# Layer 1 of a kernel's last token group by seven block products in place of eight, with its final output stored by halves

## Chip, cores and metric

One Trainium2 chip, one core. The metric is the device time in microseconds of one execution. All runs that are compared are fast; times are medians, and an interval is the 95% interval of a ratio. A ratio is the mean time of one kernel's fast runs over that of the other's in the same rounds, so it is not quite the ratio of the medians quoted.

The five engines are named as the profile names them: PE (matrix products), PEld (its weight loads), DVE (vector), ACT (scalar, activations), POOL (GpSimd) and SP (which issues most DMAs).

## The reference, cut to what matters

Windowed causal attention on 8 batches of 8 heads and 576 tokens (head size 64), then a normalised two-layer MLP with a residual:

```python
attn = softmax over a window of 64 past positions      # 8 x 8 heads x 576 x 64
x  = attn.transpose(0, 2, 1, 3).reshape(B, S, 512)
xn = (x - mean) / sqrt(var + 1e-6) * g_ln
ch = np.maximum(xn @ w_ch1, 0.0) @ w_ch2               # 512 -> 2048 -> 512
return x + ch
```

## The kernel before

The kernel works on 9 groups of 512 tokens: groups 0 to 7 are the first 512 tokens of each batch, and group 8, the tails' group, holds the last 64 tokens of all 8 batches. While PE computes the MLP of group g, the other engines prepare the attention of the following ones. "Tail i" is the attention of two batches' last 64 tokens; tails 2 and 3 are worked on in group 7. Layer 1 (`l1`) is 16 steps of four 128x512 products each; layer 2 already uses, from group 2 on, seven block products in place of eight (the Strassen-Winograd scheme), for which DVE forms sums `sS` of blocks of the hidden activations `hrT`.

```python
    ps_s = ctx.enter_context(tc.tile_pool(name="pss", bufs=2, space=PSUM))   # 2 banks
    ps_x = ctx.enter_context(tc.tile_pool(name="psx", bufs=1, space=PSUM))   # 2 banks
    ps_t = ctx.enter_context(tc.tile_pool(name="pst", bufs=1, space=PSUM))   # tags t0, t1: 2 banks
    ps_mm = ctx.enter_context(tc.tile_pool(name="psmm", bufs=2, space=PSUM)) # 2 banks
# ... cut ...
    def cast_tail(i):                      # POOL: fp32 -> fp16 of a tail's q, k, v
        # ... cut ...
        nc.gpsimd.memset(vt[:, :, :, D:D + 1], 1.0)
        nc.gpsimd.tensor_copy(out=q16, in_=tq)
        nc.gpsimd.tensor_copy(out=k16, in_=tk)
        nc.gpsimd.tensor_copy(out=vt[:, :, :, 0:D], in_=tv)
# ... cut ...
        def l1(hc):
            hps = ps_mm.tile([128, 512], FP32, tag="mm", name=f"hps_{g}_{hc}")
            for kc in range(NKC):
                nc.tensor.matmul(
                    out=hps, lhsT=w1g[:, kc, 128 * hc:128 * (hc + 1)], rhs=zT[g][:, kc, :],
                    start=(kc == 0), stop=(kc == NKC - 1),
                )
            nc.scalar.activation(out=hrT[:, hc, :], in_=hps, func=AF.Relu, bias=0.0, scale=1.0)
# ... cut: layer 2, products 1 2 6 5 7 4 3, each in two halves p; last one of the last group:
            elif n == 3:
                post("C", 0, 1)
                # ... cut ...
                if last:
                    store_rest(0, slice(256, DM), None)
# ... cut: what runs behind unit i of group g is placed with at(i, function, arguments):
        if len(TAILS.get(g, ())) == 2:     # group 7
            at(3, cast_tail, TAILS[g][1])  # POOL casts tail 3
            at(7, t_tail, TAILS[g][1], 0)  # PE transposes its q, behind layer 1's 8th step
            at(8, t_tail, TAILS[g][1], 1)  # ... and its k
```

In the traces here POOL, DVE and PE run their instructions in the order in which they are written, so a `cast_tail` that is late on POOL stops PE at its transpose, whatever else PE could do (in the changed kernel, below, for 6.87 us).

The softmax here doesn't subtract the row's maximum and nothing guards it: scores larger than these inputs give would overflow.

## Time and profile before

The time before is 314.28 us (3 runs, 313.3 to 314.37). From the page of the profile, first the engines' busy time, then the chain of waits (the work that ended last, followed back), as shares of the span by engine:

```profile
PE 298.9 (95%) x3041; PEld 194.1 (62%) x3041; DVE 205.2 (66%) x385; ACT 153.4 (49%) x258; POOL 166.3 (53%) x251
...
PE 74%; DMA 10%; DVE 7%; SPq 4%; POOL 2%; ACT 1%; issue 1%; POOLq 0%; ACTq 0%
```

PE works 95% of the time, and 74% of the chain is PE's: it is PE that the kernel mostly waits for. The chain in order of time (start, duration, engine, output tile, line, count) shows that group 7's eighth step is followed by the transposes of tail 3's q at 260.13 us, and that the tails' group is PE alone (a piece of the chain starts where the one before it ends; in PE's own timeline, from which the stretches below are taken, tpq starts at 259.97):

```profile
260.13 0.22 PE tpq L245 x4
...
281.35 13.84 PE hps L392 x64
...
305.68 1.76 PE pC L464 x16
...
307.46 0.69 DVE xn L471
```

Layer 1 of the tails' group takes 13.84 us for 64 products, 216 ns each; layer 2 takes 12.25 us for 112 narrower ones, 109 ns each. The POOL timeline (start, duration, engine, line, operation, out<-in, and in brackets the idle time before it) shows where POOL is free, and what stands at the end of that stretch:

```profile
247.81 1.04 POOL L120 CAST vt<-tv 128x1024 f16<-128x1024 f32 x1
258.43 0.17 POOL L117 MEMSET vt<- 128x16 f16 x1 [9.58 <-PE xps L317]
258.56 0.61 POOL L118 CAST tq<-tq 128x512 f16<-128x512 f32 x1
```

POOL idles 9.58 us until 258.43, and then it has 1.7 us to bring tail 3's q to PE at 260.13.

| before, profiled run | us |
|---|---|
| span | 313.0 |
| start to the first product of group 7's layer 1 | 251.99 |
| from there to the transposes of tail 3's q (tpq) | 7.98 |
| from there to the attention products of tail 3 (xps) | 7.51 |
| from there to the end of PE's last product | 39.94 |
| from there to the end (last add, stores) | 5.58 |

### The profile page before, as it was taken

To read this page: it belongs to the slowest core of one execution; us is meant where nothing else is said; L and a number is where in the kernel's file an instruction comes from. 1 tells how busy PE (TensorE), PEld (TensorE's weight loads), DVE (VectorE), ACT (ScalarE), POOL (GpSimd) and SP (SyncE) were. 2 spreads that over 40 slices of the span, in tenths; PEclk is the share of its full clock that TensorE was granted. 3 is DMA by queue.
4 is the path that set the end of the run, shared out by engine and by line. 5 is a ranking of instruction groups with operands and counts; after the bars stand their busy time and mean duration, and the time that the engine had idled before them with its cause. 6 is when DMAs were issued, how large, how long until landed. Compare 5 with 4: busy or idle time off the path is not lost.

```text
span 313.0 us, 7473 instructions
## 1 busy us (share of the span) xinstructions
PE 298.9 (95%) x3041; PEld 194.1 (62%) x3041; DVE 205.2 (66%) x385; ACT 153.4 (49%) x258; POOL 166.3 (53%) x251
## 2 busy tenths in 40 slices
PE   6988998899999999999999999999999999999992
PEld 4457544497554468646964686459646855784582
DVE  1689585855674996589666965896669636751642
ACT  1496633477416752776247526762475058306500
POOL 7578666454760798369814983698145506200000
PEclk9999999999999999999999999999999999999999
DMA  8999999998866996798179997993690393003013
GB/s 192 267 390 290 320 336 272 280 304 184 159 144 196 268 206 105 243 312 147 37 212 316 203 149 219 316 142 67 209 172 19 62 209 117 2 2 134 0 36 101
DMA packets 109892, 57.42 MB, mean 183 GB/s; under 512 B 79841, under 2 KB 100833, under 8 KB 109858
## 3 DMA queue, kind: packets, MB, share of 16 engines
q1 hardware_dynamic: 108944, 54.02, 69.1%
q0 software_dynamic: 768, 2.80, 3.7%
q8 instruction: 24, 0.39, 0.5%
q10 hardware_dynamic: 146, 0.13, 0.1%
q14 instruction: 10, 0.08, 0.1%
HBM read 38.80 MB, written 9.44 MB: 154 GB/s over the span
## 4 chain that ended last, share of the span: by engine, by line
PE 74%; DMA 10%; DVE 7%; SPq 4%; POOL 2%; ACT 1%; issue 1%; POOLq 0%; ACTq 0%
PE hps L392 30%; PE pA L464 11%; PE pC L464 7%; PE pB L464 7%; PE ch L404 6%; DMA w2s<-in_moe_w_ch_dram 4%; DMA qk<-in_k_dram 4%; PE xps L317 3%; PE sc L283 3%; PE hph L513 3%; PE tp L226 2%; SPq L141 2%; DVE sS L443 2%; DMA w1s<-in_moe_w_ch_dram 2%; SPq L89 1%; DVE pt L297 1%
## 5 line engine op out<-in xcount | busy, mean ns | idle before, releaser
L392 PE MATMUL hps<-zT,w1g 128*128 128x512 f16 x480 | 110.4, 379 | 0.0
L396 ACT ACTIVATE hrT<-hps 128x512 f16<-128x512 f32 x120 | 71.9, 599 | 50.7 <-PE hps L392 47.2
L392 PEld LDWEIGHTS <-w1g 128*128 128x128 f16 x480 | 44.6, 98 | 49.3 <-issue 1.0
L290 ACT ACTIVATE pt<-sc 128x512 f16<-128x512 f32 x72 | 39.0, 595 | 29.8 <-DVE xn L471 15.6
L464 PEld LDWEIGHTS <-sS 128*128 128x128 f16 x448 | 43.3, 98 | 5.1
L342 POOL TENSOR_SCALAR rsz<-mvg 128x1 f32<-128x1 f32 x28 | 10.7, 382 | 60.4 <-DVE mvg L328 59.8
L128 POOL CAST qk<-qk 128x1024 f16<-128x1024 f32 x32 | 35.1, 1112 | 13.4 <-DMA qk<-in_q_dram 6.9
L464 PEld LDWEIGHTS <-hrT 128*128 128x128 f16 x336 | 32.6, 98 | 5.2
L212 ACT COPY qkT<-tp 128x1024 f16<-128x1024 f16 x16 | 16.1, 1012 | 35.2 <-PE tp L226 26.1
L297 DVE TENSOR_TENSOR pt<-pt,mask 128x1024 f16<-128x1024 f16 x32 | 25.4, 800 | 11.9 <-ACT pt L290 11.9
L471 DVE TENSOR_TENSOR xn<-pA,xn 128x512 f32<-128x512 f32 x28 | 19.2, 686 | 21.1 <-PE pA L464 21.1
L443 DVE TENSOR_TENSOR sS<-hrT 128x512 f16<-128x512 f16 (+1 forms) x42 | 24.8, 591 | 10.2 <-ACT hrT L396 10.2
L464 PE MATMUL pA<-wT,sS 128*128 128x256 f16 x224 | 26.9, 273 | 0.0
L345 POOL TENSOR_SCALAR z<-xn,rsz 128x512 f16<-128x512 f32 x28 | 25.3, 902 | 2.9
L464 PE MATMUL pC<-w2s,sS 128*128 128x256 f16 x224 | 26.8, 273 | 0.0
L325 DVE BATCH_NORM_STATS2 stats<-xn 128x6 f32<-128x512 f32 x36 | 25.0, 695 | 1.2
L323 DVE TENSOR_TENSOR xn<-xps,rcp 128x512 f32<-128x512 f32 x36 | 24.9, 692 | 1.2
L513 PE MATMUL hph<-zT,w1g 128*128 128x256 f16 x192 | 23.2, 272 | 2.3 <-ACT zT L360 1.1
L320 DVE RECIPROCAL rcp<-xps 128x8 f32<-128x8 f32 x36 | 7.4, 205 | 26.8 <-PE xps L317 26.8
L404 PE MATMUL ch<-w2s,hrT 128*128 128x512 f16 x96 | 23.1, 380 | 0.0
L513 PEld LDWEIGHTS <-w1g 128*128 128x128 f16 x192 | 18.3, 98 | 5.1 <-issue 2.6
L317 PEld LDWEIGHTS <-pt 128*64 128x64 f16 x576 | 12.2, 110 | 14.4 <-issue 6.4
(85 smaller groups left out, 395.1 us busy)
## 6 DMA issues: line engine op xcount, KB each, us to landing
out_dram<-xn SPq DMA_DIRECT2D x34, 256.0 KB, 2.6
qk<-in_q_dram SPq DMA_DIRECT2D x16, 512.0 KB, 6.2
qk<-in_k_dram SPq DMA_DIRECT2D x16, 512.0 KB, 7.4
v<-in_v_dram SPq DMA_DIRECT2D x32, 256.0 KB, 6.5
w2s<-in_moe_w_ch_dram SPq DMA_DIRECT2D x12, 512.0 KB, 5.7
w1s<-in_moe_w_ch_dram SPq DMA_DIRECT2D x4, 512.0 KB, 6.7
tk<-in_k_dram SPq DMA_DIRECT2D x8, 256.0 KB, 4.7
tv<-in_v_dram SPq DMA_DIRECT2D x8, 256.0 KB, 5.3
```

The costliest lines, as they stand in the source:

```text
L128: nc.gpsimd.tensor_copy(out=dst[:, :].rearrange("p (a j) e d -> p a e j d", j=j), in_=t[:, :].rearrange("p (a e j d) -> p a e j d", e=2, j ...
L290: nc.scalar.activation(out=o, in_=i, func=AF.Exp, bias=0.0, scale=scale)
L297: nc.vector.tensor_tensor(out=ptv, in0=ptv, in1=mb, op=ALU.mult)
L323: nc.vector.tensor_tensor(out=xn, in0=xps[:, :, 0:D], in1=rcp_b, op=ALU.mult)
L325: nc.vector.bn_stats(out=stats, in_=xv)
L345: nc.gpsimd.tensor_scalar(out=z, in0=xv, scalar1=rs, scalar2=nm, op0=ALU.mult, op1=ALU.add)
L392: nc.tensor.matmul(out=hps, lhsT=w1g[:, kc, 128 * hc:128 * (hc + 1)], rhs=zT[g][:, kc, :], start=(kc == 0), stop=(kc == NKC - 1),)
L396: nc.scalar.activation(out=hrT[:, hc, :], in_=hps, func=AF.Relu, bias=0.0, scale=1.0)
L404: nc.tensor.matmul(out=ch[kb], lhsT=hrT[:, hc, 128 * kb:128 * (kb + 1)], rhs=w2s[:, hc, :], start=(hc == 0), stop=(hc == NHC - 1),)
L443: nc.vector.tensor_tensor(out=o, in0=x, in1=y, op=op)
L464: nc.tensor.matmul(out=bank[which][:, p, :], lhsT=a[:, c, 128 * p:128 * p + 128], rhs=wv[:, c, :], start=(first and p == 0 and c == 0), st ...
L513: nc.tensor.matmul(out=hps[:, e], lhsT=w1g[:, kc, 128 * hc:128 * (hc + 1)], rhs=zT[g][:, kc, 256 * half:256 * half + 256], start=(kc == 0) ...
```

## The change

The intent: layer 1 of the last group by seven block products as well, which is 1/8 less PE work there. Weights and inputs are both cut into 2x2 blocks. The sums of weight blocks (`w1S`) are formed by POOL in group 6, the sums of input blocks (`zS`) by DVE in group 7. Each of four pairs d of hidden chunks runs its seven products in PSUM banks A, B and C, skewed against the next pair. ACT copies intermediate sums out of PSUM, DVE adds, and POOL applies the relu in place. The last output stage gets one bank for each half, and each half is stored on its own.

```diff
+        def l1_product(n, d):                      # n: the product, d: the pair (0..3)
+            ...
+            if n == 1:
+                lbank[("A", d)] = ps_s.tile([128, 2, 256], FP32, tag="sc", name=f"lA_{d}")
+            elif n == 2:
+                lbank[("B", d)] = ps_t.tile([128, 2, 256], FP32, tag=f"t{d % 2}", name=f"lB_{d}")
+            elif n == 5:
+                ...                                # C: one of two banks of ps_x
+        def l1_keep(x, which, d):
+            nc.scalar.copy(out=l1_part(x, d), in_=lbank[(which, d)])
+        def l1_sum(o, which, x, d):
+            nc.vector.tensor_tensor(out=o, in0=lbank[(which, d)], in1=l1_part(x, d), op=ALU.add)
+            nc.gpsimd.tensor_scalar(out=o, in0=o, scalar1=0.0, scalar2=None, op0=ALU.max)
+        def l1_a(d):   # products 1, 2, 5
+        def l1_b(d):   # products 6, 3
+        def l1_c(d):   # product 7
+        def l1_e(d):   # product 4, then the relu on ACT, which frees bank A
+        ...
+                l1_b(0)
+                for d in range(1, 4):
+                    l1_a(d); l1_c(d - 1); l1_b(d); l1_e(d - 1)
+                    if d == 2:
+                        s_sums(0, 4, 1, 2)         # DVE: first sums of layer 2
+                stage(1, 0); l1_c(3); s_sums(4, 6, 1, 2); stage(1, 1); l1_e(3); ...
+    def w1_sums(*which):
+        ...
+            nc.gpsimd.tensor_tensor(out=o, in0=x, in1=y, op=op)     # 128 x 2048 fp16
+        if g == NGRP - 3:
+            at(22, w1_sums, 1, 2, 3, 4)            # group 6
+        if g == NGRP - 2:
+            at(22, z_sums, NGRP - 1, 1, 2)         # group 7
+            at(23, z_sums, NGRP - 1, 3, 4)
+            at(27, begin_last)                     # l1_a(0), ahead of group 7's last product
     # final stage of the last group
-                if last:
-                    store_rest(0, slice(256, DM), None)
+            if last and n == 3:
+                post_c(0, p)
+                for r in range(2):
+                    (nc.sync, nc.scalar)[r].dma_start(out=out[2 * p + r, SM:S, 256:DM], ...)
```

(Joined and cut; several statements of the plan stand on one line here.)

More of the change, by code (lines that the diff above doesn't have):

```diff
@@ L458, in product @@
             if p == 0 and n in (1, 2, 5):
-                if which == "C":
+                if which == "C" and last:
+                    for r in range(2):
+                        bank[("C", r)] = ps_t.tile([128, 256], FP32, tag=f"t{r}", name=f"pC{r}_{g}")
+                elif which == "C":
                     bank[which] = ps_t.tile([128, 2, 256], FP32, tag="t1", name=f"p{which}_{g}")
@@ L462, in product @@
                     bank[which] = ps_mm.tile([128, 2, 256], FP32, tag="mm", name=f"p{which}_{g}")
+            split_c = last and which == "C"
+            o = bank[(which, p)][:, :] if split_c else bank[which][:, p, :]
             for c in range(NHC // 2):
                 nc.tensor.matmul(
-                    out=bank[which][:, p, :], lhsT=a[:, c, 128 * p:128 * p + 128], rhs=wv[:, c, :],
-                    start=(first and p == 0 and c == 0), stop=(c == NHC // 2 - 1), skip_group_check=True,
+                    out=o, lhsT=a[:, c, 128 * p:128 * p + 128], rhs=wv[:, c, :],
+                    start=(first and (p == 0 or split_c) and c == 0), stop=(c == NHC // 2 - 1), skip_group_check=True,
                 )
@@ L471, in post, with post_c @@
             nc.vector.tensor_tensor(out=xv, in0=bank[which], in1=xv, op=ALU.add)
+        def post_c(kb0, r):
+            xv = x_norm[(g, kb0 // 2)][:, r, 256:512]
+            nc.vector.tensor_tensor(out=xv, in0=bank[("C", r)], in1=xv, op=ALU.add)
         last = g == NGRP - 1
@@ L476, in stage @@
             product(n, p)
+            if last and n == 3:
+                post_c(0, p)
+                for r in range(2):
+                    (nc.sync, nc.scalar)[r].dma_start(
+                        out=out[2 * p + r, SM:S, 256:DM],
+                        in_=x_norm[(g, 0)][64 * r:64 * r + 64, p, 256:DM],
+                    )
+                return
             if p == 0:
@@ L488, in stage @@
                 post("A", 2, 1)
-                post("C", 2, 1)
+                if last:
+                    post_c(2, 0)
+                    post_c(2, 1)
+                else:
+                    post("C", 2, 1)
                 post("A", 2, 0)
@@ L501, in stage @@
                 tbank["n"] = 0
-                if last:
-                    store_rest(0, slice(256, DM), None)
-                else:
-                    store(0)
-                    store(1)
+                store(0)
+                store(1)
         def l1_half(half, i):
@@ L533, in l2_two @@
                     add_out(kb)
+        lbank = {}
+        def l1_product(n, d):
+            w1v = w1g[:, :, :].rearrange("p (a k) (i e m) -> p a k i e m", a=2, e=2, m=128)
+            t1, t2, t3, t4 = (zS["sum"][:, m] for m in range(4))
+            z = zT[g]
+            which, a, b = {
+                1: ("A", w1v[:, 0, :, :, 0, :], z[:, 0:2, 0:256]),
+                2: ("B", w1v[:, 1, :, :, 0, :], z[:, 2:4, 0:256]),
+                5: ("C", w1S[1], t1),
+                6: ("A", w1S[2], t2),
+                3: ("C", w1S[4], z[:, 2:4, 256:512]),
+                7: ("A", w1S[3], t3),
+                4: ("A", w1v[:, 1, :, :, 1, :], t4),
+            }[n]
+            if n == 1:
[3 more added lines that the diff above has]
+            elif n == 5:
+                if "x" not in lbank:
+                    lbank["x"] = ps_x.tile([128, 2, 2, 256], FP32, tag="xps", name="lC")
+                lbank[("C", d)] = lbank["x"][:, d % 2]
+            o = lbank[(which, d)]
+            for r in range(2):
+                for kc in range(2):
+                    nc.tensor.matmul(
+                        out=o[:, r, :], lhsT=a[:, kc, 2 * d + r, :], rhs=b[:, kc, :],
+                        start=(n in (1, 2, 5) and r == 0 and kc == 0), stop=(kc == 1), skip_group_check=True,
+                    )
@@ new lines, in l1_quad, with l1_part @@
+        def l1_quad(d, e, h):
+            return hv[:, 2 * d:2 * d + 2, e, 256 * h:256 * h + 256]
+        def l1_part(x, d):
+            return zS[x][:, d % 2, :].rearrange("p (r t) -> p r t", r=2)
+        def l1_keep(x, which, d):
[3 more added lines that the diff above has]
+            nc.gpsimd.tensor_scalar(out=o, in0=o, scalar1=0.0, scalar2=None, op0=ALU.max)
@@ new lines, in l1_a @@
+        def l1_a(d):
+            l1_product(1, d)
+            l1_keep("s1", "A", d)
+            l1_product(2, d)
+            l1_sum(l1_quad(d, 0, 0), "B", "s1", d)
+            l1_product(5, d)
+            l1_keep("s5", "C", d)
+        def l1_b(d):
+            l1_product(6, d)
+            l1_keep("u2", "A", d)
+            l1_product(3, d)
+            l1_sum(l1_quad(d, 0, 1), "C", "u2", d)
+        def l1_c(d):
+            l1_product(7, d)
+            l1_sum(l1_quad(d, 1, 1), "A", "s5", d)
@@ new lines, in l1_e, with plan @@
+        def l1_e(d):
+            l1_product(4, d)
+            nc.scalar.activation(out=l1_quad(d, 1, 0), in_=lbank[("A", d)], func=AF.Relu, bias=0.0, scale=1.0)
+        if last:
+            def plan():
+                yield
+                l1_b(0)
+                for d in range(1, 4):
+                    l1_a(d)
+                    l1_c(d - 1)
+                    l1_b(d)
+                    l1_e(d - 1)
+                    if d == 2:
+                        s_sums(0, 4, 1, 2)
+                stage(1, 0)
+                l1_c(3)
+                s_sums(4, 6, 1, 2)
+                stage(1, 1)
+                l1_e(3)
+                s_sums(6, 8, 1, 2)
+                stage(2, 0)
+                stage(2, 1)
+                s_sums(0, 4, 3)
+                stage(6, 0)
+                s_sums(4, 8, 3)
+                stage(6, 1)
+                stage(5, 0)
+                s_sums(0, 4, 4)
+                s_sums(4, 8, 4)
+                stage(5, 1)
+                for n in (7, 4, 3):
+                    for p in range(2):
+                        stage(n, p)
+                yield
+            l1_a(0)
+            return plan(), s_sums
@@ L552, in mlp_units, with z_sums @@
         return units, s_sums
+    w1S = {}
+    def w1_sums(*which):
+        wv = w1g[:, :, :].rearrange("p (a k) (i e m) -> p a k i e m", a=2, e=2, m=128)
+        a11, a12, a21, a22 = (wv[:, b, :, :, a, :] for a, b in ((0, 0), (0, 1), (1, 0), (1, 1)))
+        for n in which:
+            w1S[n] = p_in.tile([128, NKC // 2, NHC // 2, 128], FP16, tag=f"qk32_{n % 2}", name=f"w1S{n}")
+            o = w1S[n][:, :, :, :]
+            x, y, op = {1: (a21, a22, ALU.add), 2: (w1S.get(1), a11, ALU.subtract),
+                        3: (a11, a21, ALU.subtract), 4: (a12, w1S.get(2), ALU.subtract)}[n]
+            nc.gpsimd.tensor_tensor(out=o, in0=x, in1=y, op=op)
+    zS = {}
+    def z_sums(g, *which):
+        if not zS:
+            t = p_in.tile([128, 4, 512], FP32, tag="v32", name="zsums", bufs=1)
+            zS["s5"] = t[:, 2:4, :]
+            zS["s1"] = p_in.tile([128, 2, 512], FP32, tag="tk32", name="s1sums", bufs=1)
+            zS["u2"] = p_in.tile([128, 2, 512], FP32, tag="tv32", name="u2sums", bufs=1)
+            zS["sum"] = t[:, 0:2, :].rearrange("p a n -> p (a n)").bitcast(FP16).rearrange(
+                "p (n k t) -> p n k t", n=4, k=2)
+        b11, b12 = zT[g][:, 0:2, 0:256], zT[g][:, 0:2, 256:512]
+        b21, b22 = zT[g][:, 2:4, 0:256], zT[g][:, 2:4, 256:512]
+        t1, t2, t3, t4 = (zS["sum"][:, n] for n in range(4))
+        for n in which:
+            o, x, y = {1: (t1, b12, b11), 2: (t2, b22, t1), 3: (t3, b22, b12), 4: (t4, b21, t2)}[n]
+            nc.vector.tensor_tensor(out=o, in0=x, in1=y, op=ALU.subtract)
     def w2_sums(i, c0, c1):
@@ L662, with begin_last @@
     load_qk(2, 1)
+    def begin_last():
+        nonlocal rest
+        rest, _ = mlp_units(NGRP - 1)
+        next(rest)
+    rest = None
     TAILS = {3: [0], 5: [1], 7: [2, 3]}
     for g in range(NGRP):
+        if g == NGRP - 1:
+            for _ in rest:
+                pass
+            break
         units, s_sums = mlp_units(g, (8, 16)[g] if g < 2 else 0, g == 0, g > 1)
```

## The prediction

> **What bounds the kernel now.** TensorE. The page gives PE 298.9 of 313.0 us busy (95%); the chain of waits is 74% PE. In the last group (the tails') the chain is PE alone: layer 1 runs 281.35 to 295.19 us (64 matmuls 128x512, 13.84 us, 216 ns each), layer 2 (already seven products) 295.19 to 307.44 (112 matmuls 128x256, 109 ns each). Then one 0.69 us add and 5 us of stores (the windows: DMA 90% busy from 308 to 311 us).
>
> **What the change removes.** 64 x 216 ns become 112 x 109 ns = 12.25 us: 1.6 us less PE work.
>
> **What it adds.** ACT: 12 copies of a PSUM bank (0.60 us) and 4 relus, for 16 relus. DVE: 12 adds (0.69 us) and four sums of z (0.42 us). POOL: 12 in-place relus (estimate 0.6 to 0.7 us) and four two-input sums of w1, 128x2048 fp16.
>
> **Walking the new layer 1** with 0.44 us per product, 0.60 us per copy, 0.69 us per add: the A bank has two buffers. The first product of pairs 2 and 3 starts right behind the fourth-product relu that frees its buffer: last matmul, 0.60 us, next matmul, so PE waits about 0.7 us twice, plus some tenths at other joins. About 1.4 of the 1.6 us are lost; net -0.1 us, perhaps +0.5. The last add shrinks from 0.69 to 0.4 us, but the stores stay DMA-bound: about -0.2 us.
>
> **The step that decides: the w1 sums on POOL.** They follow the cast of vt that ends at 248.85 us (timeline, POOL). POOL is free from there to 258.43 us (9.6 us idle). Behind it come the casts of the last tail: tq ends 259.2, and PE transposes it at 260.13 us. So the four sums have about 10.4 us, 2.6 us each. The trace has no two-input POOL instruction of any length; a cast of 2048 elements takes 1.89 us. The Trainium skill, "GPSIMD Engine Reference", 3.1, states 4497 ns for a two-input add of 2048 fp32 elements; nothing here shows it. I take the same for fp16: 4 x 4.5 = 18 us, so until about 267 us. tq is then cast at about 267.7, and PE, in order, waits about 7.5 us at the transposes of tq. The wait is long enough for the granted clock to fall: at the end of this trace it falls about 5 us after the last matmul, and at the start 512-wide matmuls take 447 ns for some 4 us before 216. That costs about 2 us more.
>
> **Sum.** 314.3 + 7.5 + 2 - 0.3 = about 323 us. If a sum takes 2.5 us or less there is no stall and the time is about 314.
>
> **What would show it.** Four POOL sums from 249 us of over 4 us each; PE idle 7 to 8 us before the transposes tpq (the waits: PE on POOL tq cast); granted clock under 1.0 in the windows after it. In the tails' layer 1: two PE waits of about 0.7 us on ACT relu; layer 1 plus 2 about 26 us in all, as before.
>
> **What would make it wrong.** A POOL sum at half the assumed time (no stall, 313 to 314.5 us); a sum of 3.4 us (stall 3 us, 317); no clock drop (321.5).
>
> Range 315.5 to 326; faster by over 2%: 0.01, within 2%: 0.33, slower by over 2%: 0.66.

## The result

326.48 us (4 runs, 325.48 to 329.07) against 313.79 us: ratio 1.0417 (1.0352 to 1.0483), slower. The result is correct. The direction was right; the time lies 0.48 us over the stated range, and the loss is 12.7 us where the terms of the prediction add up to 9.2 (314.3 + 7.5 + 2 - 0.3 is 323.5, written down as "about 323").

The page of the profile after, with the same two parts, and the group of POOL's relus (count, busy us, mean ns, idle before):

```profile
PE 300.6 (93%) x3089; PEld 199.5 (61%) x3089; DVE 219.0 (67%) x401; ACT 153.6 (47%) x258; POOL 200.3 (62%) x267
...
PE 61%; POOL 12%; DMA 10%; DVE 9%; SPq 3%; issue 2%; ACT 1%; POOLq 1%; ACTq 0%; DVEq 0%
...
L595 POOL TENSOR_SCALAR hrT<-hrT 128x512 f16<-128x512 f16 x12 | 17.5, 1485 | 11.9 <-DVE hrT L594 11.9
```

POOL now has 12% of the chain in place of 2%, and one relu takes 1485 ns. The POOL timeline from the end of the cast of vt on:

```profile
246.92 1.04 POOL L120 CAST vt<-tv 128x1024 f16<-128x1024 f32 x1
247.93 4.06 POOL L682 TENSOR_TENSOR w1S<-w1g 128x2048 f16<-128x2048 f16 x1
252.07 4.06 POOL L682 TENSOR_TENSOR w1S<-w1S,w1g 128x2048 f16<-128x2048 f16 x1
256.09 4.51 POOL L682 TENSOR_TENSOR w1S<-w1g 128x2048 f16<-128x2048 f16 x1
260.55 4.49 POOL L682 TENSOR_TENSOR w1S<-w1g,w1S 128x2048 f16<-128x2048 f16 x1
...
265.04 1.02 POOL L118 CAST tq<-tq 128x512 f16<-128x512 f32 x1
```

The four w1 sums run from 247.93 to 265.04 us, 4.06 to 4.51 us each, and only then comes the cast of tq. The waits of PE (who waited for whom: us in total, times, longest):

```profile
PE tpq L245 <- POOL tq L118: 6.9, 1, 6.9
...
PE lA L579 <- DVE hrT L594: 2.0, 1, 2.0
PE lA L579 <- ACT hrT L617: 1.4, 2, 0.7
```

PE stands still 6.9 us before tpq (6.87 in the timeline). The windows around that wait (stretch, its length, then busy us of PE, PEld, DVE, ACT and POOL, each with its count of instructions, then PEclk, the granted clock, DMA share and GB/s); the first line is of the kernel before, the others of the changed one:

```profile
260.00:270.00 10.00, 10.00 (x93) 5.58 (x92) 6.33 (x14) 7.92 (x14) 3.73 (x7) 1.00 0.06 22
...
260.00:265.00 5.00, 0.00 (x0) 0.00 (x0) 4.97 (x2) 0.00 (x0) 5.00 (x3) 0.86 0.01 6
265.00:270.00 5.00, 3.88 (x19) 2.23 (x20) 1.61 (x2) 1.86 (x3) 4.62 (x9) 0.50 0.00 0
270.00:275.00 5.00, 5.00 (x41) 2.32 (x40) 1.67 (x4) 4.04 (x9) 0.64 (x1) 0.96 0.00 0
```

From 265 to 270 us PE runs at half clock (before, the clock of this stretch was 1.00). The chain at the end of the program:

```profile
266.73 1.71 PE hps L392 x4
...
292.83 8.74 POOL hrT L595 x6
...
304.10 4.38 POOL hrT L595 x3
...
319.20 0.42 DVE xn L480
```

Four 512-wide products take 1.71 us here, 427 ns each in place of 216. In the tails' layer 1, which was PE alone before, the chain now goes through POOL's relus.

| stretch (profiled run) | before | after | difference |
|---|---|---|---|
| start to group 7's layer 1 | 251.99 | 251.11 | -0.88 |
| to tpq | 7.98 | 15.01 | +7.03 |
| to xps of tail 3 | 7.51 | 9.62 | +2.11 |
| to the end of PE's last product | 39.94 | 43.42 | +3.48 |
| to the end | 5.58 | 5.74 | +0.16 |
| span | 313.0 | 324.9 | +11.9 |

The code of the first row is the same in both kernels but for the w1 sums, of which POOL starts the first in its last 3 us; its 0.88 us is taken for scatter between executions (in six profiles with the same code up to there, those of the changed kernel, relu_dve, keep_clock, forms, sums_late and relu_fast, it runs from 250.35 to 252.43 us). The prediction had +7.5, +2, -0.1 to +0.5, and -0.2 for the other four. The fourth is the one that is off.

### The profile page after: what moved, and what is told of

It reads as the page before. It is cut to its first block, busy times and chain, and to the rows that moved or that the text cites. A ratio compares the mean times of both kernels' runs of the same rounds, so it can differ in the third digit from the quotient of the medians.

```text
span 324.9 us, 7628 instructions
## 1 busy us (share of the span) xinstructions
PE 300.6 (93%) x3089; PEld 199.5 (61%) x3089; DVE 219.0 (67%) x401; ACT 153.6 (47%) x258; POOL 200.3 (62%) x267
## 4 chain that ended last, share of the span: by engine, by line
PE 61%; POOL 12%; DMA 10%; DVE 9%; SPq 3%; issue 2%; ACT 1%; POOLq 1%; ACTq 0%; DVEq 0%
PE hps L392 22%; PE pA L469 8%; PE pC L469 6%; PE ch L404 6%; PE pB L469 5%; POOL w1S L682 4%; POOL hrT L595 4%; DMA qk<-in_q_dram 4%; PE hph L531 4%; DMA w2s<-in_moe_w_ch_dram 4%; DVE sS L443 3%; PE xps L317 3%; PE sc L283 3%; PE tp L226 2%; SPq L141 2%
## 5 line engine op out<-in xcount | busy, mean ns | idle before, releaser
L392 PE MATMUL hps<-zT,w1g 128*128 128x512 f16 x416 | 97.9, 384 | 0.0
L396 ACT ACTIVATE hrT<-hps 128x512 f16<-128x512 f32 x104 | 62.3, 599 | 40.3 <-PE hps L392 36.8
L392 PEld LDWEIGHTS <-w1g 128*128 128x128 f16 x416 | 38.8, 99 | 42.8 <-issue 2.3
L297 DVE TENSOR_TENSOR pt<-pt,mask 128x1024 f16<-128x1024 f16 x32 | 26.9, 846 | 16.7 <-ACT pt L290 16.7
L443 DVE TENSOR_TENSOR sS<-hrT 128x512 f16<-128x512 f16 (+1 forms) x41 | 25.9, 634 | 3.5 <-POOL hrT L595 2.9
L595 POOL TENSOR_SCALAR hrT<-hrT 128x512 f16<-128x512 f16 x12 | 17.5, 1485 | 11.9 <-DVE hrT L594 11.9
L531 PEld LDWEIGHTS <-w1g 128*128 128x128 f16 x192 | 18.3, 98 | 4.8 <-issue 2.2
```

The lines of the kernel that those rows point to most:

```text
L297: nc.vector.tensor_tensor(out=ptv, in0=ptv, in1=mb, op=ALU.mult)
L392: nc.tensor.matmul(out=hps, lhsT=w1g[:, kc, 128 * hc:128 * (hc + 1)], rhs=zT[g][:, kc, :], start=(kc == 0), stop=(kc == NKC - 1),)
L443: nc.vector.tensor_tensor(out=o, in0=x, in1=y, op=op)
L531: nc.tensor.matmul(out=hps[:, e], lhsT=w1g[:, kc, 128 * hc:128 * (hc + 1)], rhs=zT[g][:, kc, 256 * half:256 * half + 256], start=(kc == 0) ...
L595: nc.gpsimd.tensor_scalar(out=o, in0=o, scalar1=0.0, scalar2=None, op0=ALU.max)
```

## The experiments

Theory A: there are two separate costs. The w1 sums stand in POOL's queue ahead of the casts of tail 3, which costs a wait and then a stretch at half clock; and POOL's relus are more than twice as long as I took them for, which holds up the tails' layers. Rivals are named with each run.

The totals of relu_dve, keep_clock, relu_fast and sums_late have intervals that meet that of the changed kernel (1.0352 to 1.0483), so their gains of up to 2 us are not shown by the totals. They are read from the stretches of one profile each. What speaks for these is that up to PE's last product a stretch which an edit does not touch repeats to 0.03 us from profile to profile (to tpq: 7.98 to 7.99 us without the wait, 15.01 to 15.04 with it); stretches in which the clock falls do not.

### Taking POOL's two jobs away, one and both: w1_dve, relu_dve, both_dve

```diff
# w1_dve: the same sums on DVE, early in group 7
-            nc.gpsimd.tensor_tensor(out=o, in0=x, in1=y, op=op)
+            nc.vector.tensor_tensor(out=o, in0=x, in1=y, op=op)
-            at(22, w1_sums, 1, 2, 3, 4)                          # group 6
+            at(0, w1_sums, 1, 2); at(3, w1_sums, 3); at(6, w1_sums, 4)   # group 7
# relu_dve
-            nc.gpsimd.tensor_scalar(out=o, in0=o, scalar1=0.0, scalar2=None, op0=ALU.max)
+            nc.vector.tensor_scalar(out=o, in0=o, scalar1=0.0, scalar2=None, op0=ALU.max)
# both_dve: both edits
```

> The changed kernel with its four w1 sums on DVE, early in the group before the last, in place of POOL. Theory A (two separate costs: the w1 sums hold up the cast of tq, 6.9 us of PE wait and 2.3 us of half clock after it; the slow POOL relus hold up layer 1, 3.5 us): 9.2 us come back, about 317.3 us, no PE wait at tpq, clock 0.99 or more, but the PE wait of about 2 us for DVE hrT in layer 1 of the tails stays. Rival B (the whole loss comes from the w1 sums; the slow layer 1 is a consequence of POOL running late): 313.5 to 314.5 us and the layer-1 waits on DVE gone.

> The changed kernel with the 12 in-place relus on DVE in place of POOL; the w1 sums stay on POOL. Theory A: the 3.5 us excess of the tails' layers 1 and 2 (29.6 us from the end of group 7's own products, against 26.1 before) shrinks by 2.5 to 3.5 us, as the last sums no longer wait for POOL: about 323.3 us; the PE wait at tpq stays 6.9 us. Rival B: no change beyond 1 us (326).

> Both edits. Theory A: the two effects add: about 314 us (313.3 to 314.8), with the two PE waits of 0.7 us on ACT relu left. If the relus overload DVE, 1 us more. Rival B: the same as w1_dve within 0.5 us.

Measured, with the before kernel at 313.72 us in the same rounds: w1_dve 318.45 us (ratio 1.0156, 1.0115 to 1.0196), relu_dve 324.95 (1.0364, 1.0343 to 1.0386), both_dve 316.80 (1.0104, 1.0087 to 1.0121).

w1_dve takes back 8.0 us: the wait at tpq is gone (7.99 us to it, as before), and the wait of 2.0 us for DVE hrT in the tails' layer 1 stays. So rival B falls: the slow layer 1 does not come from POOL being late. It is 1.15 us over the expectation. In its profiled run, the slowest of the four, the clock fell at another place, inside the tails' layer 1, behind that 2 us wait (to half from 297.7 to 301.2 us):

```profile
295.00:300.00 5.00, 3.02 (x19) 2.22 (x18) 2.56 (x5) 0.92 (x2) 3.92 (x4) 0.78 0.00 0
300.00:305.00 5.00, 4.97 (x40) 4.01 (x39) 4.25 (x8) 0.60 (x1) 2.38 (x2) 0.88 0.01 3
```

In the profile of the changed kernel these windows show a clock of 1.00, though PE waits there just as long (1.97 us). But the run of forms below, which is the changed kernel up to its last group's end, has that wait of 1.97 us too, and behind it the clock was at half from 306.7 to 310.0 us; its stretch from xps to PE's end is 44.50 us, like the 44.51 of w1_dve and not like the 43.42 of the changed kernel. The clock fell there in two of the four profiles that have this wait (not in those of the changed kernel and of keep_clock), and in none of the eight of the new layer 1 that lack it. So the slow relus seem to bring a second cost of about 1.1 us, in some executions and not in others. The four runs of w1_dve, 317.02, 317.86, 319.05 and 320.15 us, have mean granted clocks of 0.998, 0.995, 0.994 and 0.989: this fits, but is no test of it.

relu_dve takes back 1.5 us by the medians and 1.96 us in its stretch (41.46 against 43.42), with the wait at tpq unchanged at 6.9 us. That is theory A's direction, but less than the 2.5 to 3.5 us expected. both_dve is 2 us over the top of its expectation: its stretch xps to PE's end is 41.46 us, exactly that of relu_dve, and 1.5 us over the kernel before. So something else was left in layer 1; see free_banks.

### The clock: keep_clock

```diff
             at(3, cast_tail, TAILS[g][1])
+            at(7, keep_warm, 32)      # 32 dummy 512-wide products on PE; its definition is cut
             at(7, t_tail, TAILS[g][1], 0)
```

> The changed kernel with 32 dummy 512-wide matmuls (6.9 us) on PE in the place where it waits for tq, nothing else. Theory A's clock term (the wait lets the granted clock fall, which costs 2.3 us after it): PE reaches tpq at the same time, granted clock stays 1.0 in the windows behind it, 2.0 to 2.5 us come back: about 324.2 us. Rival (the slow stretch after the wait has another cause, such as z of the tails arriving late from POOL): 326.5 us, unchanged.

Measured: 324.84 us (ratio 1.0375, 1.0328 to 1.0422). The same windows:

```profile
260.00:265.00 5.00, 5.00 (x25) 2.24 (x23) 4.97 (x3) 0.00 (x0) 5.00 (x3) 1.00 0.01 3
265.00:270.00 5.00, 4.81 (x45) 2.27 (x44) 0.88 (x1) 3.47 (x6) 4.55 (x7) 1.00 0.00 0
```

PE reaches tpq after 15.04 us (15.01 in the changed kernel), so the dummy products cost nothing; the clock stays at 1.00, and the stretch behind takes 7.88 us in place of 9.62. So the fall of the clock behind the wait costs about 1.7 us, a little less than the 2.0 to 2.5 expected; the rival (the slow stretch has another cause) falls, as the stretch and the clock show. What is left over the 7.51 us of the kernel before, 0.37 us, was not looked into.

### What a relu on POOL costs, and why: forms, relu_fast, sums_late

forms adds, behind the last group, three rounds of nine POOL instructions on 512 elements a partition, on scratch tiles.

```diff
+        P.tensor_scalar(out=d1, in0=fb, scalar1=0.0, scalar2=None, op0=ALU.max)          # L986: as the relu
+        P.tensor_scalar(out=d2, in0=fl, scalar1=0.0, scalar2=None, op0=ALU.max)          # L987: contiguous
+        P.tensor_scalar(out=d2, in0=d2, scalar1=0.0, scalar2=None, op0=ALU.max)          # L988: in place
+        P.tensor_scalar(out=d1, in0=fb, scalar1=1.0, scalar2=None, op0=ALU.mult)         # L989
+        P.tensor_scalar(out=d1, in0=fb, scalar1=1.0, scalar2=0.0, op0=ALU.mult, op1=ALU.max)  # L990
+        P.tensor_scalar(out=d1, in0=fa, scalar1=0.0, scalar2=None, op0=ALU.max)          # L991: fp32 input
+        P.tensor_scalar(out=d1, in0=fa, scalar1=1.0, scalar2=0.0, op0=ALU.mult, op1=ALU.add)  # L992: fp32 input
+        P.tensor_copy(out=d1, in_=fb)                                                    # L993
+        P.tensor_tensor(out=d1, in0=fb, in1=..., op=ALU.add)                             # L994
```

> The changed kernel, with three rounds of nine POOL instructions behind its last group, on 512 elements a partition, on scratch tiles: which part of the relu's form makes it take 1.46 us where a two-operation fp16-from-fp32 instruction of the same size takes 0.76. Theory C: the max operation is what is slow: every form with max is 1.3 us or more, and the in-place, contiguous, fp32-input and multiply forms tell it apart (multiply and copy 0.6 to 0.8 us). Rival D: fp16 input with an immediate is slow whatever the operation: multiply on fp16 also 1.4 us, fp32-input max 0.7 us. Rival E: being in place is slow: only that form is 1.4 us. A two-input add of 512: about 1.1 us if 4.06 us at 2048 scales.

The last of the three rounds (DVE idle by then), POOL's timeline:

```profile
340.61 1.48 POOL L986 TENSOR_SCALAR d<-w1g 128x512 f16<-128x512 f16 x1
...
343.63 1.48 POOL L988 TENSOR_SCALAR d<-d 128x512 f16<-128x512 f16 x1
345.08 1.49 POOL L989 TENSOR_SCALAR d<-w1g 128x512 f16<-128x512 f16 x1
346.65 1.92 POOL L990 TENSOR_SCALAR d<-w1g 128x512 f16<-128x512 f16 x1
348.66 1.49 POOL L991 TENSOR_SCALAR d<-xn 128x512 f16<-128x512 f32 x1
350.23 0.62 POOL L992 TENSOR_SCALAR d<-xn 128x512 f16<-128x512 f32 x1
350.91 0.61 POOL L993 COPY d<-w1g 128x512 f16<-128x512 f16 x1
351.61 1.15 POOL L994 TENSOR_TENSOR d<-w1g 128x512 f16<-128x512 f16 x1
```

Neither theory C nor the rivals D and E hold. Every form with one operation and an immediate takes 1.48 to 1.49 us: the maximum with fp16 or fp32 input, contiguous (L987, also 1.48 us) or not, in place or not, and the multiply (fp16 input only). Multiply-then-add takes 0.62 us (fp32 input here, 0.66 with fp16 in relu_fast below), a copy 0.61, multiply-then-max 1.92. (A profile's spans on POOL are rough; but the starts of these instructions are 1.45 to 1.57, 0.68, 0.70 and 2.01 us apart, which bears them out.) What in the form makes it slow stays open. My estimate of 0.6 to 0.7 us for the relu had been carried over from casts (0.61 us for 512 elements) and from the multiply-add that makes z (0.76), and those are the two quick forms. A two-input add costs 1.15 us for 512 elements, so 2.2 ns an element, and 4.06 us for 2048, 2.0 ns an element.

relu_fast puts the quick form in the relu's place. The result is wrong (it is no relu any more), but engine, count, order and waits are the same.

```diff
-            nc.gpsimd.tensor_scalar(out=o, in0=o, scalar1=0.0, scalar2=None, op0=ALU.max)
+            nc.gpsimd.tensor_scalar(out=o, in0=o, scalar1=1.0, scalar2=0.0, op0=ALU.mult, op1=ALU.add)
```

> The changed kernel with POOL's in-place maximum replaced by times 1 plus 0, the form that took 0.62 us in the run of forms: a wrong result on purpose, the same engine, count, order and waits, only the duration differs. My prediction had 0.6 to 0.7 us for it. Theory A (the duration of the relu is the mis-sized term): the tails' layers 1 and 2 take about 27.5 us in place of 29.6, the 1.97 us wait for DVE hrT shrinks under 0.5 us, the rest (6.9 us at tpq, the clock) stays: about 324.3 us, near my prediction's 322.8. Rival K (it is POOL's hand-over, not its duration): 326 us, waits unchanged.

Measured: 324.25 us (ratio 1.0316, 1.0273 to 1.0358). The group of the twelve instructions, from the list of groups, and the waits of PE from 240 us on:

```profile
L595 POOL TENSOR_SCALAR hrT<-hrT 128x512 f16<-128x512 f16 x12 | 7.9, 658 | 17.6 <-DVE hrT L594 17.6
```

```profile
PE tpq L245 <- POOL tq L118: 6.9, 1, 6.9
PE lA L579 <- ACT hrT L617: 1.4, 2, 0.7
```

658 ns each, and the wait for DVE hrT is gone. The stretch xps to PE's end is 40.84 us, 2.6 us less than with the real relu and 0.9 us over the kernel before. So it is the duration of the relu and nothing about handing over; rival K falls. With the duration that I had assumed, the time comes out at 324.25 us, near the 323.5 to which the prediction's terms add up (the 322.8 of the expectation stands nowhere in the prediction).

How a POOL instruction comes to stop PE: DVE's first sums of layer 2 (`sS`) need relus that are still queued on POOL, and DVE works in order, so the sums of the last pair stand behind them. From the timeline of the changed kernel, all engines:

```profile
292.83 10.18 POOL L595 TENSOR_SCALAR hrT<-hrT 128x512 f16<-128x512 f16 x7 [1.56 <-DVE hrT L594]
...
301.60 1.09 DVE L443 TENSOR_TENSOR sS<-hrT 128x1024 f16<-128x1024 f16 x1 [1.91 <-POOL hrT L595]
...
303.33 0.68 DVE L594 TENSOR_TENSOR hrT<-lB,s1sums 128x512 f16<-128x512 f32 x1
...
304.67 0.60 PE L579 MATMUL lA<-zsums,w1g 128*128 128x256 f16 x4 [1.97 <-DVE hrT L594]
```

DVE idles 1.91 us for POOL, then does its sums late, and PE's product 4 of pair 2 waits 1.97 us for it. sums_late tests whether this order is the whole of it:

```diff
-                    if d == 2:
-                        s_sums(0, 4, 1, 2)
+                s_sums(0, 4, 1, 2)     # behind the loop over the pairs
                 stage(1, 0)
```

> The changed kernel with DVE's first two sums of layer 2 (which wait for POOL's relus) put behind the sums of the last pair, so that they block nothing. Theory F (the PE wait of 1.97 us for DVE hrT is DVE's order; but POOL, at 12 x 1.46 us in a 12 us stage, is what bounds it): the 1.97 us wait goes, a wait of about 1 us for POOL hrT appears in layer 2's first product or in the last sums, net gain 0.5 to 1.2 us. Rival G (the order is all of it): the 3.5 us excess of the tails' layers falls by 2 us and no new wait appears.

Measured: 326.77 us (ratio 1.0388, 1.0341 to 1.0435): no gain. The 1.97 us wait is gone, but PE now waits 0.66 us for POOL's relu itself, and 0.87 us in place of 0.35 for the last sums; its stretch is 0.70 us shorter (42.72). That much is theory F; rival G falls. The net gain that F forecast, 0.5 to 1.2 us, does not show in the total. In the profiled run the stretch behind tpq, at half clock, took 10.24 us in place of 9.62, which uses up most of the 0.70. That stretch took 9.4 to 10.3 us in the five profiles that have the wait and no dummy products.

### Only the place in POOL's queue: w1_split

From relu_dve: the same four sums, still on POOL, two of them later: POOL ends the second at 255.85 us, goes on to the casts, and takes up the other two at 271.06.

```diff
-            at(22, w1_sums, 1, 2, 3, 4)      # group 6
+            at(22, w1_sums, 1, 2)            # group 6
+            at(15, w1_sums, 4, 3)            # group 7, behind POOL's last z
```

> relu_dve (324.95) with the same four w1 sums still on POOL, two left where they are and two moved 20 us later, behind POOL's last z. Theory A (the cost is the position in POOL's queue): the wait at tpq and the fall of the clock go, minus 9 us. Theory J (POOL and DVE shut each other out while one runs a two-input instruction): the two late sums meet DVE's sums of group 7 and the z sums: some of these take 2 to 4 us in place of 0.4, and PE waits 1 to 3 us in layer 2 of group 7 or at the first product with z sums: in all 317 to 319 us. Without J: 316 us or less.

Measured: 318.60 us (ratio 1.0154, 1.0131 to 1.0177), 6.35 us under relu_dve. The wait at tpq and the half clock are gone (7.98 and 7.51 us, as before): the cost was the place in the queue. And theory J holds. DVE's sums beside the two late w1 sums, and what PE waited for:

```profile
271.84 3.56 DVE L443 TENSOR_TENSOR sS<-hrT 128x512 f16<-128x512 f16 x1
...
275.93 3.67 DVE L443 TENSOR_TENSOR sS<-hrT,sS 128x512 f16<-128x512 f16 x1
```

```profile
PE pC L469 <- DVE xn L476: 1.4, 1, 1.4
...
PE pA L469 <- DVE xn L476: 1.1, 1, 1.1
```

Each of these two sums takes 0.41 to 0.42 us where POOL is idle. They end, at 275.40 and 279.60 us, just behind the POOL sums that end at 275.12 and 279.32. The changed kernel has the same thing: a DVE sum of 0.69 us took 4.42 us beside the fourth w1 sum, but PE was standing still there anyway.

The Trainium skill, "SBUF — State Buffer", "SBUF: two separate sides", says that a DVE instruction with two SBUF inputs and a POOL instruction that reads SBUF shut each other out: whichever starts first keeps the ports that they share for its whole instruction. These runs agree, with the numbers above, and the reverse shows too: in the changed kernel the cast of tq took 1.02 us in place of 0.61 beside the DVE sum of 4.42 us, which ended at 265.60.

### What is left in layer 1: free_banks, best, best2

The chain of both_dve in the tails' layer 1, one turn of it:

```profile
287.51 0.61 PE lA L579 x4
...
288.20 0.59 ACT s1sums L591
...
288.82 0.70 DVE hrT L594
...
289.55 0.29 DVE hrT L595
289.84 0.61 DVE hrT L594
...
290.49 0.61 PE lA L579 x4
...
291.13 0.61 ACT hrT L617
...
291.77 0.61 PE lA L579 x4
```

Product 1 of pair 2, ACT's copy, DVE's add, relu and add, product 4 of pair 1, ACT's relu, and then product 1 of pair 3, which needs the bank that this relu frees. From 287.51 to 291.77 one turn takes 4.26 us, where PE has 3.06 us of work in a pair (seven products of 0.44 us). free_banks gives the A sums two more banks:

```diff
-                lbank[("A", d)] = ps_s.tile(...)
+                pool, tag = (ps_s, "sc") if d < 2 else (ps_mm, "mm")
+                lbank[("A", d)] = pool.tile(...)
# layer 2 of the last group: banks A and B from ps_s in place of ps_mm
```

> both_dve with two more PSUM banks for the A sums: pairs 2 and 3 take the two banks that layer 1 leaves unused, and layer 2's A and B take the two that pairs 0 and 1 freed. Theory H (with POOL out of the way, what is left of the loss in layer 1 is a ring: product 1, ACT copy, two DVE adds, product 4, ACT relu, and only then product 1 two pairs on, because the A bank has two buffers; 4.26 us a pair in the trace of both_dve where PE needs 3.06): the 0.7 us waits on ACT hrT vanish, 1.5 to 2.2 us come back against both_dve: about 315.0 us. Rival I (DVE, at about 2.9 us a pair plus its layer-2 sums, is the bound, not the banks): less than 0.7 us comes back and the waits move to DVE hrT.

Measured: 314.87 us (ratio 1.0035 to the kernel before, 1.0012 to 1.0058), 1.9 us under both_dve by the medians, 1.0 us in its stretch (40.47 us). The waits on ACT hrT vanish. A wait of 0.89 us on DVE hrT appears. So the ring was there, but the stretch got back less than theory H's 1.5 us and more than rival I's 0.7: 1.4 us of waiting on ACT went, and DVE's order took part of that back. Where the other 0.9 us of the medians comes from, the stretches do not show.

> free_banks, with the w1 sums on DVE moved to its idle stretches before POOL's casts start (so that z of the tails is not delayed and PE does not wait 0.4 us for it), and the final stage as before (not stored by halves). By theories A and H the rest of the loss goes: 313.6 to 314.4 us, even with the kernel before; a gain of 0.5 us if the DVE chain hides better than I think. A clear gain over 1 us is not expected: seven products save 1.6 us in all and about 1 us of joins stays.

```diff
# best, on free_banks
-            at(0, w1_sums, 1, 2); at(3, w1_sums, 3); at(6, w1_sums, 4)             # group 7
+            at(22, w1_sums, 1); at(23, w1_sums, 2)                                 # group 6
+            at(0, w1_sums, 3, 4)                                                   # group 7
# and the final stage as in the kernel before
```

Measured: 315.69 us (ratio 1.0060, 1.0033 to 1.0088), a miss. The wait for z is gone (7.51 us from tpq to xps, as before), but I had put two sums into DVE's queue in group 6 ahead of an add that PE then waited 0.92 us for.

> free_banks with three things mended that its trace and that of best show: the fourth w1 sum at a place where both DVE and POOL are idle (no two-input instructions against each other), the final stage as before, and DVE's first sums of layer 2 behind the last pair's sums so that product 4 of pairs 1 and 2 does not wait (0.24 and 0.89 us there). Theory H: about 1.2 us against free_banks (0.4 for z, 0.2 to 0.3 for the stores, 0.5 for the sums): 313.4 to 314.0 us, 0 to 0.5 us under the kernel before. If it is no faster than free_banks, the remaining loss is not in the waits I named.

```diff
# best2, on best
-            at(22, w1_sums, 1); at(23, w1_sums, 2)                                 # group 6
-            at(0, w1_sums, 3, 4)                                                   # group 7
+            at(0, w1_sums, 1, 2); at(3, w1_sums, 3); at(13, w1_sums, 4)            # group 7
-                    if d == 2:
-                        s_sums(0, 4, 1, 2)
+                s_sums(0, 4, 1)
                 stage(1, 0); l1_c(3)
+                s_sums(0, 4, 2)
```

Measured: 313.52 us against 314.29 (ratio 0.9978, 0.9949 to 1.0007): not clear of noise, so a gain is not shown. Its profile agrees: the four stretches sum to 60.93 us, those of the kernel before to 61.01. So even with the costs named above mended the change gains nothing that these runs can show. Its stretch xps to PE's end is 39.86 us against 39.94: the 1.6 us of saved products are spent on joins between PE, ACT and DVE. PE's timeline shows it: where the starts of PE's groups lie further apart than their products need (109 ns each, as in the kernel before), the excess adds up to 1.53 us in this stretch, against 0.02 in the kernel before. It sits at seven places, all in the last group: 0.30 us before product 5 of pair 1, 0.11, 0.40 and 0.36 before product 4 of pairs 0, 1 and 2, and 0.36 in all at three places where layer 2 begins. The profile names a releaser for two of them only, DVE's sums, with waits of 0.24 and 0.20 us.

### The final stage alone: tail_only

The kernel before with only the last part of the change.

```diff
+                    for r in range(2):
+                        bank[("C", r)] = ps_t.tile([128, 256], FP32, tag=f"t{r}", ...)
...
-                    store_rest(0, slice(256, DM), None)
+            if last and n == 3:
+                post_c(0, p)      # add, then two DMAs, for each half p
```

> The kernel before with only the last part of the change: the final output stage in two banks, stored by halves. My prediction's term: minus 0.2 us at best, the stores being bound by DMA: 313.3 to 314.0, not clear of noise. Rival: the shorter last add shows in full and the halves overlap: minus 0.6 us or more. Second rival: SP's two more issues cost time: plus 0.3 us.

Measured: 314.73 us against 314.42 (ratio 1.0013, 0.9984 to 1.0041). No effect of the total within noise. In the profile, PE's last product to the end is 5.83 us, against 5.58, and the table below repeats this: 5.73 to 5.88 us in the ten kernels that store by halves, 5.58 in each of the three that do not. So the halves lengthen the end by 0.15 to 0.3 us, which is too little for the totals to show; that is the direction of the second rival, but that SP's issues are the reason was not tested.

### All stretches side by side

Profiled runs; the columns are the four stretches of the table above.

| kernel | to tpq | to xps | to PE's end | to the end | median us |
|---|---|---|---|---|---|
| before | 7.98 | 7.51 | 39.94 | 5.58 | 313.79 |
| the change | 15.01 | 9.62 | 43.42 | 5.74 | 326.48 |
| w1_dve | 7.99 | 8.06 | 44.51 | 5.77 | 318.45 |
| relu_dve | 15.02 | 9.42 | 41.46 | 5.87 | 324.95 |
| both_dve | 7.98 | 8.06 | 41.46 | 5.88 | 316.80 |
| keep_clock | 15.04 | 7.88 | 43.44 | 5.79 | 324.84 |
| relu_fast (wrong result) | 15.02 | 10.17 | 40.84 | 5.73 | 324.25 |
| sums_late | 15.03 | 10.24 | 42.72 | 5.84 | 326.77 |
| w1_split | 7.98 | 7.51 | 44.36 | 5.86 | 318.60 |
| free_banks | 7.98 | 8.07 | 40.47 | 5.79 | 314.87 |
| best | 7.98 | 7.51 | 40.47 | 5.58 | 315.69 |
| best2 | 7.98 | 7.51 | 39.86 | 5.58 | 313.52 |
| tail_only | 7.99 | 7.51 | 39.94 | 5.83 | 314.73 |

The stretches move one by one: each edit changes the stretch that it should and leaves the others alone, apart from the clock and from 0.55 us behind tpq in w1_dve, both_dve and free_banks, where PE waits 0.4 us for the tails' z. (w1_dve's third entry includes the fall of its clock. The medians are from several sessions, in which the kernel before had 313.7 to 314.4 us.)

## Why the prediction was right in its direction and wrong in its size

- **The w1 sums on POOL: right, the figure in part by luck.** Predicted 4.5 us each, a wait of about 7.5 us at tpq. Measured 4.06, 4.06, 4.51 and 4.49 us and a wait of 6.87 us. w1_dve and w1_split remove it, once by moving the engine and once by moving the place alone. The figure came from the Trainium skill, "GPSIMD Engine Reference", 3.1, which gives 4497 ns for an fp32 add of this length; the trace of the kernel before had no number for the step (its only two-input POOL instruction, L343, works on one element a partition). That these sums are fp16 was left out of account: alone they took 4.06 us, and the two that took 4.5 started while a two-input DVE instruction was still running.
- **The clock: right, in part by luck.** Predicted about 2 us. keep_clock gives 1.7 us, by the stretch behind the wait; over the profiles with the wait that stretch is 1.9 to 2.8 us longer than before. The clock fell between 263 and 264 us, some 4 us after PE's last product at 259.25, much as the trace before shows at its end. The other ground, how long half speed lasts, was misread: at the start of the trace before, 512-wide products still take 0.43 us or more at 12 us, 9 us after PE's first product.
- **The relus on POOL: the step that failed.** The prediction put it as "12 in-place relus (estimate 0.6 to 0.7 us)" and from that took "net -0.1 us, perhaps +0.5" for the tails' layers. Measured: 1.49 us each, 17.5 us of POOL work in a stage that was to last 12 us, and +3.48 us in the stretch that holds these layers. relu_fast, with the same instructions at 0.66 us, has +0.90. So the mis-sized term is the duration of one POOL form, 0.65 assumed and 1.49 measured, and it was worth 2.6 us, or, as an estimate from the stretches of w1_dve and forms, 3.7 where the clock falls behind the 2 us wait.
- **The ring in layer 1: the waits right, their sum too small.** Predicted two PE waits of about 0.7 us on ACT's relu; measured 0.73 and 0.69. "About 1.4 of the 1.6 us are lost" was short: with quick relus (relu_fast) the tails' layers still stand 0.9 us over the kernel before, so all of the 1.6 us and 0.9 us more are lost. In PE's timeline these 2.5 us are 1.73 around the two waits and 0.78 at other joins, which the prediction had as "some tenths". The forecast of the total was off by this too, by 0.4 to 1 us.
- **The final stage: no gain.** Predicted -0.2 us; the totals of tail_only show no effect, the profiles +0.15 to +0.3.

The profile's difference of 11.9 us is 7.0 us of wait, 2.1 us behind it at the lower clock, 3.5 us of layers and 0.2 us of end, less 0.9 us of scatter at the start; the prediction's sum had 7.5, 2.0, -0.1 and -0.2.

## What to carry to other kernels

An engine that idles 9.6 us is not free for any 9.6 us of work: cost the work in the form in which it will run, and look at what stands behind it in the same queue. A duration measured for one instruction form of an engine doesn't carry over to another of the same size: on POOL a copy, a multiply-add, a maximum and a two-input add of 512 elements took 0.61, 0.62, 1.48 and 1.15 us. Before saving products in a chain that is pure PE, walk the sums around them, ring by ring through the PSUM banks: here 1.6 us of saved products met 1.53 us of joins even in the best of the kernels.

## What the Trainium skill lacked or had wrong

- "GPSIMD Engine Reference", 4.1 (engine selection), says that one-input elementwise work is roughly line-rate. Here that held for a copy (0.61 us for 512 elements) and for multiply-then-add (0.62), not for one operation with an immediate: maximum (fp16 or fp32 input) and multiply (fp16) took 1.48 to 1.49 us, and multiply-then-max 1.92. No page lists the POOL forms by speed.
- "GPSIMD Engine Reference", 3.1, has the two-input add only in fp32 (4497 ns for 2048). In fp16 it took 4.06 us, and 4.49 to 4.51 us where a two-input DVE instruction was still running at its start: fp16 gains little.
- "TensorE: Matmul & The Clock Gate", Part 1, has a table of two clock states, half and full, and says that an idle window of about 3.4 us makes the clock fall. The trace agrees in the wait of 6.87 us (427 ns for a 512-wide product in place of 216, back to full some 4 us after the wait). But the clock also fell to half for some 3.4 us behind PE waits of only 1.98 us (w1_dve) and 1.97 us (forms), shorter than that window, and it did not behind the same 1.97 us in the profile of the changed kernel. The page's "second HAM failure mode" speaks of micro-idles that are frequent enough, but gives no length or share of idle time at which that begins.
